# Half of a stage's matrices on other engines, and wider products, in a convolution with a fused feed-forward block

## The chip, the cores and the metric

The kernel runs on one core of a Trainium2 chip. Five engines work from their own instruction queues: PE (TensorE, matrix products into PSUM; its weight loads are shown as PEld), DVE (VectorE), ACT (ScalarE), POOL (GpSimd) and SP (SyncE), which here issues all transfers. A queue is worked in order; an instruction that waits holds up all behind it. The metric is the device time of one launch in microseconds (us), median of five runs.

## The reference

A long convolution, and a feed-forward block on its result (shapes: 4 batches, 12480 positions, 128 channels; 2048 hidden units; all float32):

```python
h_filt = (np.maximum(pos_emb @ w1, 0.0) @ w2) * np.exp(-0.01 * pos)[:, None]
u = x * v
y = irfft(rfft(u, n=2*S) * rfft(h_filt, n=2*S)[None])[:, :S]
x1 = (x * y).reshape(B*S, D)
h = x1 @ w_in
out = (h * np.cos(h)) @ w_out
```

## The kernel before

The transform of a batch is done in steps of matrix products: u = x * v and sums of it (u_units), a first step (f1_units, 64 blocks of two channels each), a second step with 48 pairs of matrices w, each followed by the product with the filter's transform (f2_units), and an inverse in two steps (i1_units, i2_units). Generators hand out pieces of this work, and `units` (L514) interleaves them: in the unit j it issues `before(j + ahead)`, the products of j, and the pieces of `after(j - 1)`.

The order of the opening, written out at L784 and below:

- The filter: 11 pieces of pos_emb are scaled (DVE, L331), turned and put through the first layer; then 30 times `filter_out` (two matmuls, a copy on ACT at L356, two sums on DVE at L359 into ftile). x * v of the first batch (first_u) is drawn along: a load of x and v (SP), the product in two halves on POOL or DVE (u_multiply, L390), and two sums, one on POOL and one on DVE (L396). x has three buffers, v two; v's buffer is free when both halves are done.
- f1 of the filter: 64 blocks of two matmuls (L402) whose results ACT or DVE evicts (f1_evict_filter; `share` is ACT's part), six pieces of which go by for each unit of first_u while that lasts. Afterwards the tables for the way back are made (inverse_tables: POOL makes the angles at L190 to L217, ACT the sines at L226, one step for every five pieces of f1) and stored.
- f1 of the first batch, beside which w_in is converted from 64-bit floats (L133 to L156).
- f2_both_units: each of the 48 pairs makes two matrices w, of the form even0 * a + even1 * b (`turn`: ACT makes the first term in a PSUM bank at L289, DVE multiplies and adds at L291), multiplies them with the batch and with the filter (L442, L445, L448), copies the filter's result to SBUF as h (ACT, L614), and multiplies by it: four products on DVE (L458, L460) and two sums on POOL (L461). w and h are stored to DRAM (wd, hd; SP) and read again for the other batches. w has two buffers, h three; w is made one pair ahead.
- i1 of the first batch, beside which w_out is converted and some of the matrices of the last step are made.

Then the main loop starts: the feed-forward block (L727 to L758) with the rest of the convolution drawn along, a piece whenever its share is due.

Of the kernel before, what the change touches and what calls it, by code (L numbers as in the profile page):

```python
# [30 lines left out]
def kernel(  # L31
# [46 lines left out]
    nc = tc.nc  # L78
# [30 lines left out]
    dram = ctx.enter_context(tc.tile_pool(name="dram", bufs=1, space=DRAM))  # L109
    hd = dram.tile([N1 // 2, N2, 2, 2, D], F32, name="hd")  # L110
    zd = dram.tile([NROWS, G, D], F32, name="zd")
# [140 lines left out]
    def inverse_tables(pool):  # L252

        t = Tables(pool, nc.gpsimd, 4)
        part = t.whole([P, 1], [[1, 1]], channel_multiplier=1, name="part")
        part4 = t.whole([P, 1], [[1, 1]], base=1, channel_multiplier=4, name="part4")
        step = t.whole([P, P], [[1, P]], name="step")
        mid = t.whole([P, P], [[1, P]], base=-MID, name="mid")
        cs, rows, tw_t = back_tables(pool)
        yield from t.sines(step, part, N2, [(cs[:, 0, 0:H + 1], 1), (cs[:, 1, 0:H + 1], 0)],  # L260
                           eighths=slice(0, H + 1, H))
        yield from t.sines(step[:, 1:H], part, N2,
                           [(cs[:, 0, H + 1:], 0), (cs[:, 1, H + 1:], 1)])
        yield from t.sines(step, part4, 4 * N1,
                           [(rows[:, i, :], q) for i, q in enumerate((0, 1, 2, 3))])
        yield from t.sines(mid, part4, TURN, [(tw_t[:, 0, :], 1), (tw_t[:, 1, :], 0)],
                           eighths=slice(H - 1, N2, H))
        t.finish(len(t.waiting))
        for kept, made in ((csd, cs), (rowsd, rows), (twd, tw_t)):
            nc.sync.dma_start(kept[:, :, :], made[:, :, :])  # L270

    def back_tables(pool):

        cs = pool.tile([N2, 2, N2], F32, name="cs")
        rows = pool.tile([N1, 4, R], F32, name="rows")

        tw_t = pool.tile([N1, 2, N2], F32, name="tw_t")
        return cs, rows, tw_t

# [157 lines left out]
    def f2_mm(ps, w, k1, i, filt=False):  # L437

        k = k1 + i
        pi = ps[0:N2, i * 2 * D:(i + 1) * 2 * D]  # L440
        if not filt:
            nc.tensor.matmul(pi, w[:, i, :], parts[0:KE, :, k], start=True, stop=True)  # L442
        elif k < KF:
            both = ftile[0:KE, :, k:k + N1 + 1:N1, :].rearrange("p b r i -> p r b i")
            nc.tensor.matmul(pi, w[:, i, :], both, start=True, stop=True)  # L445
        else:
            for r, src in enumerate((ftile[0:KE, :, k, :], above[0:KE, :, k - KF, :])):
                nc.tensor.matmul(pi[:, r * D:(r + 1) * D], w[:, i, :], src,  # L448
                                 start=True, stop=True)

    def f2_product(pool, ps, h, k1):

        y = parts[0:N2, :, k1:k1 + 2, :, :].rearrange("p r k b i -> p r b k i")
        uu, hh = (a.rearrange("p g r (b i) -> p r b g i", i=2) for a in (
            ps[0:N2, :].rearrange("p (g r d) -> p g r d", g=2, r=2), h[:, :, :, :]))
        t = pool.tile([N2, 2, CB, 2, 2], F32, name="t", bufs=1)
        for r, op in ((0, ALU.subtract), (1, ALU.add)):
            nc.vector.tensor_tensor(y[:, r], uu[:, 0], hh[:, r], op=ALU.mult)  # L458
            yield
            nc.vector.tensor_tensor(t[:, r], uu[:, 1], hh[:, 1 - r], op=ALU.mult)  # L460
            nc.gpsimd.tensor_tensor(y[:, r], y[:, r], t[:, r], op=op)  # L461
            yield
# [82 lines left out]

    def u_units(b, bufs, u, engine, side="left"):

        with tc.tile_pool(name="xv", bufs=bufs, side=side) as pool:
# [5 lines left out]
            def after(j, _):  # L554
                for half in range(2):
                    u_multiply(tiles[j], half, engine(j, half))
                    yield
                if j == H // UA - 2:
# [3 lines left out]

            yield from units(H // UA, U_STEPS, before, lambda j, ps, i: None, after, 3,
                             ahead=bufs - 2)

# [9 lines left out]
    def f2_units(bank):  # L575
        with tc.tile_pool(name="there", bufs=3) as pool:
            ws, hs = {}, {}

            def before(j):
                ws[j] = pool.tile([KE, 2, N2], F32, name="w")  # L580
                nc.sync.dma_start(ws[j][:, :, :], wd[j, :, :, :])
                hs[j] = pool.tile([N2, 2, 2, D], F32, name="h")
                nc.sync.dma_start(hs[j][:, :, :, :], hd[j, :, :, :, :])

            def mm(j, ps, i):
                if i == 0:
# [4 lines left out]
            yield from units(N1 // 2, F2_STEPS, before, mm,  # L591
                             lambda j, ps: f2_product(pool, ps, hs.pop(j), 2 * j), 4)

    def f2_both_units(bank):

        with tc.tile_pool(name="both", bufs=2) as pool:
            ws = {}

            def before(j):
                ws[j] = pool.tile([KE, 2, N2], F32, name="w")  # L600
                for i in range(2):
                    make_w(ws[j][:, i, :], 2 * j + i, half=bank)
                nc.sync.dma_start(wd[j, :, :, :], ws[j][:, :, :])
# [8 lines left out]
            def after(j, ps):  # L612
                h = pool.tile([N2, 2, 2, D], F32, name="h", bufs=3)
                nc.scalar.activation(h[:, :, :, :].rearrange("p g r d -> p (g r d)"),  # L614
                                     ps[1][0:N2, :], AF.Copy, scale=1.0 / M)
                nc.sync.dma_start(hd[j, :, :, :, :], h[:, :, :, :])
                yield from f2_product(pool, ps[0], h, 2 * j)

            yield from units(N1 // 2, F2_STEPS, before, mm, after, 4, ahead=1)

# [163 lines left out]
    with tc.manual_schedule():  # L784
        with tc.tile_pool(name="psum", bufs=8, space=PSUM) as psum, \
# [14 lines left out]
            with tc.tile_pool(name="layers", bufs=1, side="right") as pool:  # L800
# [8 lines left out]
                for i in range(1, NCH):  # L809
                    pes[i] = filter_load(pool, i)  # L810
                first_u = u_units(0, 3, slots[0:R, :, :, :],
                                  lambda j, half: nc.vector if half and j % 3 and j < 18
                                  else nc.gpsimd)
                next(first_u)
# [6 lines left out]
                for i in range(NCH + 1):  # L821
# [6 lines left out]
                    next(sines, None)  # L828
                    if i >= 4:
                        for _ in range(2):  # L830
                            next(first_u)
                for _ in sines:
# [5 lines left out]
            with tc.tile_pool(name="out", bufs=1, side="right") as pool:  # L838
                for j in range(H // 2):
                    filter_out(pool, bank, aT, ftile, j, w2_sb)  # L840
                    for _ in range(1 + (j % 3 == 0)):
                        next(first_u)
            f1 = f1_units(bank, ftile[0:FR, :, :, :], 0.53, f1_evict_filter)
            for _ in first_u:
                for _ in range(2):
                    next(f1)
# [26 lines left out]
            lpool = ctx.enter_context(tc.tile_pool(name="late", bufs=1))  # L873
            cs, rows, tw_t = back_tables(lpool)
            for kept, here in ((csd, cs), (rowsd, rows), (twd, tw_t)):
                nc.sync.dma_start(here[:, :, :], kept[:, :, :])
            for _ in f2_both_units(bank):
                pass
            first.close()

            wpool = ctx.enter_context(tc.tile_pool(name="weights", bufs=1))
            ident = wpool.tile([P, P], F32, name="ident")
            make_identity(nc, ident)
# [91 lines left out]
```

## Time and profile before

| | us |
|---|---|
| median of 5 runs | 3785.89 |
| the runs | 3781.93 to 3787.73 |
| profiled execution: device time | 3785.22 |
| its span, first to last instruction | 3783.4 |
| f1 of the filter begins | 64.09 |
| x * v of the first batch ends on POOL | 97.41 |
| f1 of the first batch: ACT's last eviction ends | 169.37 |
| i1 of the first batch begins | 272.83 |
| main loop's first feed-forward matmul | 345.29 |

In the lines of the profile, "out<-in" are the program's names of the tiles, then partitions x elements, "x" the number of instructions, busy time and the mean of one. The idle time of an engine is given with what ended it. "Busy" of PE is modelled, since matmuls are pipelined.

### The profile page before, as it was taken

The numbers are of one execution on the slowest core, as the hardware profiler recorded it, in microseconds if no ns is written. First come the engines' busy times: TensorE is split into PE (matmuls) and PEld (weight loads), VectorE is DVE, ScalarE is ACT, GpSimd is POOL, SyncE is SP. The second block draws the span as 40 slices with busy tenths as digits, with TensorE's granted clock in tenths as the row PEclk, the third lists the DMA queues.
The fourth block names the chain that finished last, engine by engine and source line by source line (L and its number), as shares of the span: only waits on it lengthen the run. The fifth ranks groups of instructions, "written<-read, shape, count | busy, mean of one in ns | idle before, by whom it ended". The sixth has DMA issues, their size and how long they took to land.

```text
span 3783.4 us, 47244 instructions
## 1 busy us (share of the span) xinstructions
PE 3701.4 (98%) x13546; PEld 2109.2 (56%) x13546; DVE 2769.3 (73%) x5658; ACT 2523.9 (67%) x4683; POOL 2588.6 (68%) x2342
## 2 busy tenths in 40 slices
PE   7898999999999999999999999999999999999999
PEld 6777555655466555555565556555566544444444
DVE  7887887688866777788766786788765566666666
ACT  5757776766665557666655567666664677777777
POOL 7667886588854665688745664788644577777776
PEclk9999999999999999999999999999999999999999
DMA  6253552022202650122103540122105200000000
GB/s 166 71 177 105 148 148 57 18 71 79 74 18 67 179 159 27 34 77 78 57 18 110 174 125 17 52 78 76 41 12 167 87 20 20 17 20 20 17 21 14
DMA packets 209500, 276.14 MB, mean 73 GB/s; under 512 B 17112, under 2 KB 146536, under 8 KB 209112
## 3 DMA queue, kind: packets, MB, share of 16 engines
q1 hardware_dynamic: 209239, 273.12, 24.9%
q8 instruction: 109, 1.79, 0.2%
q14 instruction: 152, 1.24, 0.1%
HBM read 193.64 MB, written 79.42 MB: 72 GB/s over the span
## 4 chain that ended last, share of the span: by engine, by line
PE 84%; POOL 7%; DVE 4%; ACT 2%; DMA 2%; issue 2%; SPq 0%; POOLq 0%; DVEq 0%; ACTq 0%
PE ph L727 31%; PE acc L752 27%; PE cv L752 5%; PE cv L491 5%; PE cv L466 4%; POOL f L736 4%; PE cv L402 3%; PE cv L442 3%; PE ph L126 2%; PE ps L402 1%; PE ps L442 1%; DMA tm<-td 1%; PE ps L466 1%; POOL tm L295 1%; DVE k L733 1%
## 5 line engine op out<-in xcount | busy, mean ns | idle before, releaser
L736 POOL TENSOR_TENSOR f<-a,k 128x512 f32<-128x512 f32 (+1 forms) x1568 | 1984.9, 1266 | 1054.2 <-DVE k L733 1053.2
L727 PE MATMUL ph<-at,w_in_sb 128*128 128x512 f32 (+1 forms) x3136 | 1599.9, 591 | 5.8 <-DVE gt L743 5.2
L730 ACT ACTIVATE a<-ph,quarter 128x512 f32<-128x512 f32 (+1 forms) x1568 | 1072.4, 684 | 760.7 <-PE ph L727 752.3
L752 PE MATMUL acc<-gt,w_out_sb 128*128 128x512 f32 (+1 forms) x2688 | 1374.4, 593 | 9.9 <-ACT ot L758 9.3
L743 DVE TENSOR_TENSOR gt<-ph,cs 128x512 f32<-128x512 f32 (+1 forms) x1568 | 1078.0, 687 | 317.2 <-ACT cs L741 289.2
L733 DVE TENSOR_SCALAR k<-a 128x512 f32<-128x512 f32 (+1 forms) x1568 | 769.1, 490 | 621.4 <-ACT a L730 604.1
L741 ACT ACTIVATE cs<-f 128x512 f32<-128x512 f32 (+1 forms) x1568 | 980.3, 625 | 329.3 <-POOL f L736 326.9
L752 PEld LDWEIGHTS acc<-gt,w_out_sb 128*128 128x128 f32 x2688 | 506.4, 189 | 662.3 <-issue 619.3
L727 PEld LDWEIGHTS ph<-at,w_in_sb 128*128 128x128 f32 x3136 | 554.4, 190 | 337.6 <-issue 267.2
L461 POOL TENSOR_TENSOR slots<-slots,t 120x256 f32<-120x256 f32 x384 | 311.3, 817 | 60.8 <-DVE t L460 38.8
L491 PEld LDWEIGHTS cv<-slots,tm 96*104 96x104 f32 x1920 | 239.8, 170 | 110.8 <-issue 79.9
L491 PE MATMUL cv<-slots,tm 96*104 96x128 f32 x1920 | 254.4, 275 | 10.8 <-DVE tm L291 4.9
L752 PE MATMUL cv<-gt,w_out_sb 128*128 128x512 f32 (+1 forms) x448 | 224.6, 584 | 0.7 <-DVE gt L743 0.7
L466 PEld LDWEIGHTS cv<-cs,slots 120*96 120x96 f32 x1536 | 176.8, 167 | 67.5 <-issue 65.6
L466 PE MATMUL cv<-cs,slots 120*96 120x120 f32 x1536 | 183.2, 266 | 0.0
L442 PE MATMUL cv<-slots,w 124*120 124x256 f32 x576 | 173.2, 381 | 0.0
L442 PEld LDWEIGHTS cv<-slots,w 124*120 124x120 f32 x576 | 103.7, 184 | 123.7 <-issue 110.8
L402 PEld LDWEIGHTS cv<-c,slots 104*124 104x124 f32 x768 | 132.6, 192 | 71.1 <-issue 58.3
L402 PE MATMUL cv<-c,slots 104*124 104x192 f32 x768 | 151.3, 327 | 4.8 <-DVE gt L743 3.5
L752 PEld LDWEIGHTS cv<-gt,w_out_sb 128*128 128x128 f32 x448 | 85.0, 190 | 104.4 <-issue 99.4
L390 DVE TENSOR_TENSOR xt<-xt,vt 104x256 f32<-104x256 f32 x177 | 138.8, 791 | 0.2
L476 DVE TENSOR_TENSOR slots<-cv,other 96x240 f32<-96x240 f32 x384 | 133.4, 393 | 4.2 <-ACT other L474 4.2
(129 smaller groups left out, 2579.3 us busy)
## 6 DMA issues: line engine op xcount, KB each, us to landing
h<-hd SPq DMA_DIRECT2D x144, 240.0 KB
tm<-td SPq DMA_DIRECT2D x96, 312.0 KB
xt<-in_x_dram SPq DMA_DIRECT2D x120, 208.0 KB
vt<-in_v_dram SPq DMA_DIRECT2D x120, 208.0 KB
xs<-in_x_dram SPq DMA_DIRECT2D x120, 208.0 KB
zd<-zs SPq DMA_DIRECT2D x119, 208.0 KB
zb<-zd SPq DMA_DIRECT2D x96, 256.0 KB
w<-wd SPq DMA_DIRECT2D x144, 116.2 KB
```

Source lines behind the costliest of these rows:

```text
L402: nc.tensor.matmul(ps[0:KE, i * 2 * N1:(i + 1) * 2 * N1], u[:, b, 0:KE, i], c1[0:u.shape[0], :, :].rearrange("p r k -> p (r k)"), start=Tr ...
L442: nc.tensor.matmul(pi, w[:, i, :], parts[0:KE, :, k], start=True, stop=True)
L461: nc.gpsimd.tensor_tensor(y[:, r], y[:, r], t[:, r], op=op)
L466: nc.tensor.matmul(ps[0:N1, (i * 2 + r) * N2:(i * 2 + r + 1) * N2], parts[0:N2, r, :, b, i], cs[:, r, :], start=True, stop=True)
L491: nc.tensor.matmul(ps[0:R, i * D:(i + 1) * D], t[:, i, r, :], slots[0:N1, :, place, :], start=(r == 0), stop=(r == 1))
L727: nc.tensor.matmul(ph[:, 0:m], w_in_sb[:, c * P:(c + 1) * P], ats[n][:, 0:m], start=True, stop=True)
L730: nc.scalar.activation(a[:, 0:m], ph[:, 0:m], AF.Identity, bias=quarter[:, 0:1], scale=INV_TWO_PI)
L733: nc.vector.tensor_scalar(out=k[:, 0:m], in0=a[:, 0:m], scalar1=ROUND, scalar2=ROUND, op0=ALU.add, op1=ALU.subtract)
L736: nc.gpsimd.tensor_tensor(f[:, 0:m], a[:, 0:m], k[:, 0:m], op=ALU.subtract)
L741: nc.scalar.activation(cs[:, 0:m], f[:, 0:m], AF.Sin, scale=TWO_PI)
L743: nc.vector.tensor_tensor(gt[:, 0:m], ph[:, 0:m], cs[:, 0:m], op=ALU.mult)
L752: nc.tensor.matmul(accs[n][:, 0:m], w_out_sb[:, c, :], gt[:, 0:m], start=(c == 0), stop=(c == NFC - 1))
```

## The change

In f2_both_units, the second matrix of each pair is made without DVE: ACT makes both terms in SBUF (the second in a tile `spare`), and POOL adds them. Matrices are made two pairs ahead instead of one, with three buffers of w; h has two buffers instead of three. The two halves of the product are one instruction each: the real part of the batch (or the imaginary part) is read twice, by a step of zero, and multiplied with both parts of h in one product of 512 elements; for this, the results of both matrices of a pair lie interleaved in PSUM and in h, so that the four elements of a pair of matrices and a pair of channels are neighbours. f2_units for the other batches keeps four products of 256, in the new layout. t has two buffers in the first case.

In first_u, the product x * v is one instruction for a unit (104x512) in place of two; DVE does those of the units 15, 19, 23 and 27, POOL the others (before, DVE did twelve halves among the first 18 units). The places where first_u is drawn are spread differently, and ACT's share of the filter's f1 is 0.58 instead of 0.53. The tables rows and tw_t for the last step are read back from DRAM after f2_both_units instead of ahead of it.

```diff
-        pi = ps[0:N2, i * 2 * D:(i + 1) * 2 * D]
+        pi = ps[0:N2, :].rearrange("p (r b g i) -> p g r b i", r=2, g=2, i=2)[:, i]
...
-    def f2_product(pool, ps, h, k1):
+    def f2_product(pool, ps, h, k1, whole):
+        y = parts[0:N2, :, k1:k1 + 2, :, :].rearrange("p r k b i -> p r b (k i)")
+        t = pool.tile([N2, 2, CB, 4], F32, name="t", bufs=1 + whole)
+        uu = ps[0:N2, :].rearrange("p (r b j) -> p r b j", r=2, j=4)
+        if whole:
+            for r, (dst, hh) in enumerate(((y, h[:, :, :, :]), (t[:, :, :, :], h[:, ::-1, :, :]))):
+                u = uu[:, r]
+                twice = bass.AP(tensor=u.tensor, offset=u.offset,
+                                ap=[u.ap[0], [0, 2], *u.ap[1:]])
+                nc.vector.tensor_tensor(dst, twice, hh, op=ALU.mult)
+                yield
         for r, op in ((0, ALU.subtract), (1, ALU.add)):
-            nc.vector.tensor_tensor(y[:, r], uu[:, 0], hh[:, r], op=ALU.mult)
-            yield
-            nc.vector.tensor_tensor(t[:, r], uu[:, 1], hh[:, 1 - r], op=ALU.mult)
+            if not whole:
+                nc.vector.tensor_tensor(y[:, r], uu[:, 0], h[:, r], op=ALU.mult)
+                yield
+                nc.vector.tensor_tensor(t[:, r], uu[:, 1], h[:, 1 - r], op=ALU.mult)
             nc.gpsimd.tensor_tensor(y[:, r], y[:, r], t[:, r], op=op)
             yield
...
-                for half in range(2):
+                for half in (0, 1) if halves else (slice(0, 2),):
                     u_multiply(tiles[j], half, engine(j, half))
...
     def f2_both_units(bank):
...
-                ws[j] = pool.tile([KE, 2, N2], F32, name="w")
-                for i in range(2):
-                    make_w(ws[j][:, i, :], 2 * j + i, half=bank)
+                ws[j] = pool.tile([KE, 2, N2], F32, name="w", bufs=3)
+                spare = pool.tile([KE, N2], F32, name="spare")
+                make_w(ws[j][:, 1, :], 2 * j + 1, spare=spare[:, :])
+                yield
+                make_w(ws[j][:, 0, :], 2 * j, half=bank)
+                yield
                 nc.sync.dma_start(wd[j, :, :, :], ws[j][:, :, :])
...
-                h = pool.tile([N2, 2, 2, D], F32, name="h", bufs=3)
+                h = pool.tile([N2, 2, CB, 4], F32, name="h")
...
-            yield from units(N1 // 2, F2_STEPS, before, mm, after, 4, ahead=1)
+            yield from units(N1 // 2, F2_STEPS, before, mm, after, 4)
...
-                                  lambda j, half: nc.vector if half and j % 3 and j < 18
-                                  else nc.gpsimd)
+                                  lambda j, half: nc.vector if j >= 15 and j % 4 == 3
+                                  else nc.gpsimd, halves=False)
...
-                    if i >= 4:
-                        for _ in range(2):
-                            next(first_u)
+                    if i >= 2:
+                        next(first_u)
...
-                    for _ in range(1 + (j % 3 == 0)):
+                    if j % 3:
                         next(first_u)
-            f1 = f1_units(bank, ftile[0:FR, :, :, :], 0.53, f1_evict_filter)
+            f1 = f1_units(bank, ftile[0:FR, :, :, :], 0.58, f1_evict_filter)
             for _ in first_u:
-                for _ in range(2):
+                for _ in range(3):
                     next(f1)
...
-            cs, rows, tw_t = back_tables(lpool)
-            for kept, here in ((csd, cs), (rowsd, rows), (twd, tw_t)):
-                nc.sync.dma_start(here[:, :, :], kept[:, :, :])
+            cs = third_table(lpool)
+            nc.sync.dma_start(cs[:, :, :], csd[:, :, :])
             for _ in f2_both_units(bank):
                 pass
             first.close()
             wpool = ctx.enter_context(tc.tile_pool(name="weights", bufs=1))
+            rows, tw_t = last_tables(wpool)
+            for kept, here in ((rowsd, rows), (twd, tw_t)):
+                nc.sync.dma_start(here[:, :, :], kept[:, :, :])
```

## The prediction

> **What bounds the kernel now.** I read the shares of each engine, the chain that ended last by line, busy time by stretch, and in the opening the waits and the order in time.
>
> ```profile
> PE 3701.4 (98%) x13546; PEld 2109.2 (56%) x13546; DVE 2769.3 (73%) x5658; ACT 2523.9 (67%) x4683; POOL 2588.6 (68%) x2342
> ```
>
> PE is full, and from 339 us on the chain is almost all PE. Apart from the layout of the products, the change touches only the first 339 us, so what it wins must be won there. Busy time by stretch (length, PE, PEld, DVE, ACT, POOL, clock, DMA share, GB/s):
>
> ```profile
> 31.20:64.09 32.89, 26.11 (x120) 19.52 (x121) 30.21 (x83) 11.04 (x30) 27.47 (x32) 0.95 0.59 173
> 64.09:97.40 33.31, 33.05 (x180) 32.45 (x180) 29.39 (x96) 25.52 (x113) 28.72 (x39) 0.90 0.51 145
> 97.40:120.28 22.88, 15.13 (x80) 12.80 (x80) 20.47 (x77) 11.99 (x52) 19.27 (x51) 0.96 0.04 13
> 120.28:169.37 49.09, 43.54 (x252) 42.62 (x252) 39.94 (x108) 44.06 (x133) 29.46 (x32) 0.95 0.23 67
> 205.00:267.00 62.00, 60.23 (x332) 48.01 (x332) 57.88 (x181) 36.70 (x88) 42.12 (x61) 1.00 0.61 176
> ```
>
> The filter's last layer (31 to 64) hangs on DVE, the next stretch on DVE and PE, the one from 97 on POOL, the one from 120 on ACT (44 of 49 us). Why from 97 on POOL, the order in time shows:
>
> ```profile
> 119.82 0.43 POOL L217 TENSOR_TENSOR turned<-moved,turned 96x120 f32<-96x120 f32 x1
> 120.28 0.30 ACT L226 ACTIVATE tw_t<-turned 96x120 f32<-96x120 f32 x1 [1.89 <-POOL turned L217]
> ...
> 121.80 4.45 PE L402 MATMUL ps<-c,slots 104*124 104x192 f32 x15 [7.05 <-ACT slots L410]
> ```
>
> POOL ends x * v of the first batch at 97.41, needs 22.8 us for the inverse tables, ACT waits for its last sine until 120.28, and PE stood 7.05 us behind ACT. So the end of x * v on POOL sets all that follows to 169.37.
>
> In the second step (f2_both_units, 169.4 to 272.8) DVE looks like the bound. But here is one pair:
>
> ```profile
> 207.27 0.24 SPq L603 DMA_DIRECT2D wd<-w  x1
> ...
> 208.67 0.59 DVE L291 SCALAR_TENSOR_TENSOR w<-even,tw_w,ps 124x120 f32<-124x120 f32 x2
> ...
> 209.29 0.24 SPq L603 DMA_DIRECT2D wd<-w  x1
> ...
> 210.68 0.59 DVE L291 SCALAR_TENSOR_TENSOR w<-even,tw_w,ps 124x120 f32<-124x120 f32 x2
> ```
>
> The store of w issued at 207.27 has its last completion at 210.56, and the matrix that reuses its buffer starts at 210.68; the store from 205.25 completes at 208.55, its successor starts at 208.67. From the sixteenth pair on the gap is 0.12 to 0.13 us nearly every time, which is also the gap after the visible stalls. So the stores hold the stage, whatever DVE does. In the trace's completions a store of w has one at 0.41 us and four at 2.7 to 3.3; a store of h one at 0.54 and fifteen at 2.4 to 3.6. A store of w thus runs on four DMA engines: 31 of its 124 packets each, one every 0.040 us; a store of h on fifteen, 8 packets each, one every 0.084. On the slowest engine w completes 1.38 after the h before it, and h 0.63 after the w before it: 2.01 us a pair, against 2.02 between issues. The mean DMA share of 0.61 hides this.
>
> [...]
>
> **The change, part by part.**
>
> *x * v with one product a unit.* POOL had 48 half products of 0.71 (34.1 us uncontended), DVE 12. Now 26 whole ones on POOL, 4 on DVE. No 104x512 product of two SBUF tiles is in this stage; nearest is POOL's 128x512 subtraction at 1.266 (33 us for 26), on DVE 104x512 at 0.680. So POOL hardly gains in work; DVE loses 12 x 0.41 and gains 4 x 0.68. What moves is the pace: in the last layer (30 filter_out) only 10 units come instead of 13. DVE there: 60 x 0.35 + 10 x 0.41 = 25 us, below PE's 26; so that layer takes 26 to 27 us plus the last pair's 1.3. It starts 0.6 earlier (one sum of u less stands between the filter's scalings), so f1 of the filter starts at about 58.5 instead of 64.09. But x * v itself runs at its own pace: load of v 3.05 us after its issue (86.31 to 89.40), then the product, two buffers: (3.1 + 1.3) / 2 = 2.2 us a unit at least, 2.35 with DVE's share (three evictions x 0.42 x 1.38 + a sum 0.43 + a quarter product), against 2.43 now. The sixteenth sum falls near 63.2 instead of 64.6, thirteen more units give 93.8, POOL's end 94.7: **-2.7** (bounds 0, same cadence, to -5, at 2.2).
>
> *Tables.* Same POOL work, so ACT resumes at 117.8. Only 7 of the sine steps are now placed among the filter's evictions, so these are done by then (two, 2.4 us of ACT, were left before), and ACT is free of sines; the other sines stand ahead of the first batch's evictions on ACT, and PE can run nine blocks ahead of them (eight banks) before it stops, as now. What ACT still has: 35 blocks x 1.06 + 8 conversions x 0.84 = 43.8, plus 2 idle (2.9 before): first step done at 163.6 instead of 169.3, **-5.7 together** (0 to -8). Share 0.58 instead of 0.53 is in these sums.
>
> *Second step.* Engines, per pair: DVE 2 x 0.68 + 0.335 = 1.70 by rows (six instructions, 2.34, spaced to 2.02 before); ACT 0.60 + 3 x 0.355 = 1.67; POOL 2 x 0.73 + one 124x120 sum, 0.43 by L217's 96x120, = 1.89; PE 1.75. All under 2.01, so the stores decide. Counted from ACT's end of the first step, E: the first store goes at E+1.4 (before E+1.0: a third ACT instruction), its packets 1.4 later; three stores of w follow at once, then the pipeline fills (PE 3.5 us to the first h, as now), and from the fifth w at E+10.6 the four engines are always fed: 44 x 1.38 + 43 x 0.63 = 87.8, E+98.4. Disturbed pairs add what they add now, 2.0 (intervals 2.49, 2.70, 2.29 and the like over 2.02). The last h needs the store two before it (two buffers instead of three), which lies behind the last w: 0.63 + 0.09 + copy 0.6 + products 1.3 + two sums 1.4 = 4.1. E+104.5; before 272.83 - 169.33 = 103.5. **+1** (bounds -7, if the packets alone counted, 1.91 a pair; +21, rival two). The waits of DVE on w (5.0 us in all) go; DVE's on POOL for t (1.6) too; h on its store is next, and behind it on ACT stand the three instructions of the w three pairs later, which has two pairs of slack. wd now waits for POOL and DVE on SP, and hd stands behind it; both have over 0.25 us in hand before the engines run dry.
>
> *Moved loads.* rows and tw_t are issued after the last h has landed, 0.3 us into the inverse step, ahead of w_in_sb and the raw pieces. They land 2.39 and 2.19 after issue; the first reader is ACT at 276.91, 4.1 in. w_in_sb and raw come 0.8 later; raw landed at 279.4 and DVE reads it at 282.23. **0**; without this cover, 1.2.
>
> *Layout.* PE now writes PSUM in runs of two elements; no matmul here does that. Reading runs of two from SBUF costs nothing: 256 columns of L442 come every 0.435, 1.70 ns each, as with L727's contiguous 512. The write side lies between 0 and a doubling; I take 0, as the reading row. The product over four contiguous elements stays at DVE's one-element pace (0.417), **0**.
>
> Sum: -5.7 + 1 = -4.7 on the profiled execution's 3785.22 (span 3783.4 and 1.8 around it): 3780.5. That execution is 0.67 under the median of the five runs, so for the median **3781**.
>
> **Rivals.**
> 1. *The stores are hidden.* The stage follows the packets (1.91) and the start fills sooner: 44 x (2.07 - 1.91) = -7, with the opening 3772.5. For: DVE is 93% busy. Against: the 0.12 us gap, the 1.38 between completions also when two w follow each other unblocked at the start.
> 2. *Slower: two buffers of h.* A pair takes at least (0.6 copy + 0.05 + landing + 0.09) / 2. Landing alone is 2.50 (1.6 a pair), behind w 3.58 (2.17, +5: 3784.5), at worst 4.29 (2.52, +21: 3800). It decides against the kernel by 0.2% from 3.95 on. Against it: between two stores of h that share a buffer the four engines have 3.4 us of other work anyway, so waiting adds nothing unless they idle.
> 3. *Strided PSUM writes cost PE.* Batches two to four have 288 such matmuls, 125 us: 10% is +12.5, 3793.5. Nothing in the trace speaks for it, nor excludes it.
> 4. *No change*: x * v keeps 2.43 a unit and the tables end at 120: 3784 to 3787.
>
> **How the numbers follow.** Forecast 0.58 (own range 3776 to 3786), rival one 0.17, two 0.13, three 0.05, four 0.07. The measurement tells 0.2%, 7.6 us: faster means under 3778.3. That holds for nearly all of rival one and a quarter of the forecast's cases: 0.30; slower, over 3793.5: two's upper part and three, 0.10; same 0.60. The range 3770 to 3790 leaves out rival one's best and the slower cases.
>
> **What would show it.** f1 of the filter starting near 58.5; the last IOTA on POOL near 95; ACT's first w at 163.6; intervals of wd still 2.01 to 2.05 with DVE idle in them; the inverse step starting near 268. Wrong if intervals of wd fall to 1.9 (one), if ACT waits on hd with the intervals over 2.2 (two), or if L442 in the later batches lengthens (three).

## The result, and the profile after

The changed kernel takes 3793.06 us (median of 25 runs, 3788.39 to 3797.04) against 3786.25 for the kernel before (43 runs beside it): 6.8 us longer, a ratio of 1.0016 with a 95% interval of 1.0011 to 1.0022. The forecast was 3781, its range ended at 3790. The profiled execution took 3795.57, with a span of 3793.8; it is one of the longer ones.

The first row of the page of the changed kernel: VectorE lost 17 us of work and 172 instructions, GpSimd and ScalarE gained 13 each.

```profile
PE 3704.2 (98%) x13546; PEld 2112.6 (56%) x13546; DVE 2752.0 (73%) x5486; ACT 2537.3 (67%) x4751; POOL 2601.9 (69%) x2368
```

Busy time by stretch (length, PE, PEld, DVE, ACT, POOL, clock, DMA share, GB/s); the borders are the same events as before, but for 107.00: x * v ends on GpSimd at 105.0 and its first table instruction starts at 106.43.

```profile
33.98:62.88 28.90, 26.13 (x121) 19.57 (x121) 26.86 (x70) 11.04 (x30) 21.77 (x21) 0.99 0.46 133
62.88:107.00 44.12, 40.93 (x223) 39.17 (x224) 41.89 (x119) 35.05 (x155) 27.08 (x33) 0.93 0.49 142
107.00:129.23 22.23, 10.87 (x63) 9.74 (x61) 13.40 (x47) 9.16 (x39) 18.69 (x47) 0.88 0.04 12
129.23:176.17 46.94, 41.39 (x228) 40.21 (x228) 37.54 (x102) 41.81 (x122) 29.46 (x32) 0.90 0.24 71
205.00:267.00 62.00, 60.22 (x318) 46.78 (x317) 46.00 (x91) 42.46 (x121) 54.83 (x91) 1.00 0.59 178
```

The filter's last layer is 4 us shorter, but starts 2.8 us later. From there to GpSimd's first table instruction it is 43.6 us where it was 33.4, with VectorE busy in 95% of that stretch. The tables, from that instruction to the last sine, take what they took (22.8 us, 22.8 before), and what follows a little less (46.9, 49.1 before), only later. The second step shows the idle VectorE that was forecast (46.0 of 62 us; 57.9 before), and no speed from it. The order in time shows what the late tables bring:

```profile
129.23 0.30 ACT L226 ACTIVATE tw_t<-turned 96x120 f32<-96x120 f32 x1 [1.89 <-POOL turned L217]
129.56 0.31 SPq L270 DMA_DIRECT2D twd<-tw_t  x1
130.64 5.80 PE L404 MATMUL ps<-c,slots 104*124 104x192 f32 x17 [11.98 <-ACT slots L412]
131.28 1.31 SPq L173 DMA_DIRECT2D raw<-in_moe_w_in_dram  x3
134.81 0.29 DVE L133 TENSOR_SCALAR power<-raw 128x256 uint32<-128x256 uint32 x1 [13.96 <-DMA raw<-in_moe_w_in_dram]
```

The last sine ends 9 us later than before (120.28), TensorE stands 12.0 us behind ScalarE instead of 7.1, and VectorE, which did not wait there before, stands 14.0 us for the raw words of the feed-forward weights, whose loads come behind the tables' stores. The first batch's first step ends at 176.17 on ScalarE instead of 169.37. From there to the first matmul of the third step it is 106.1 us (103.5 before); from that matmul to the end 3511.5 (3510.6). So nearly all of the loss arises ahead of the third step.

### The profile page after: what moved, and what is told of

It reads as the page before. It is cut to its first block, busy times and chain, and to the rows that moved or that the text cites. A ratio compares the mean times of both kernels' runs of the same rounds, so it can differ in the third digit from the quotient of the medians.

```text
span 3793.8 us, 47221 instructions
## 1 busy us (share of the span) xinstructions
PE 3704.2 (98%) x13546; PEld 2112.6 (56%) x13546; DVE 2752.0 (73%) x5486; ACT 2537.3 (67%) x4751; POOL 2601.9 (69%) x2368
## 4 chain that ended last, share of the span: by engine, by line
PE 81%; POOL 7%; DVE 4%; DMA 3%; ACT 2%; issue 2%; SPq 0%; POOLq 0%; DVEq 0%; ACTq 0%
PE ph L740 31%; PE acc L765 26%; PE cv L765 5%; PE cv L501 4%; PE cv L476 4%; POOL f L749 4%; PE cv L404 3%; PE cv L445 3%; PE ph L126 2%; DMA tm<-td 1%; DMA hd<-h 1%; POOL slots L471 1%; PE ps L476 1%; ACT cs L754 1%; POOL tm L297 1%
## 5 line engine op out<-in xcount | busy, mean ns | idle before, releaser
L471 POOL TENSOR_TENSOR slots<-slots,t 120x256 f32<-120x256 f32 x384 | 311.1, 816 | 32.7 <-DVE t L470 16.5
L486 DVE TENSOR_TENSOR slots<-cv,other 96x240 f32<-96x240 f32 x384 | 133.5, 393 | 4.1 <-ACT other L484 4.1
L392 DVE TENSOR_TENSOR xt<-xt,vt 104x256 f32<-104x256 f32 (+1 forms) x169 | 133.8, 799 | 0.3 <-DMA vt<-in_v_dram 0.3
```

## The experiments

The opening theory: x * v of the first batch ends later, and tables, raw words and first step with it. The rival: the second step makes the loss. This table holds, for one profiled execution of each kernel, the first matmul of the filter's last layer, of the filter's first step, the last matmul of batch 0's first step, the first of the second and of the third step; then the difference of the medians to the runs of the kernel before on the same chip. An opening varies from one execution to the next: in the five kernels with the whole new opening (changed, e2, e4, e6, e7) batch 0's first step ends at 166.6 to 172.1. The profiled execution also need not be a typical one: it lies 2.5 us above the median of its kernel's runs in the changed kernel and 3.0, 3.9 and 5.3 below it in e2, e3 and e4. So single rows tell less than groups.

| kernel | last layer | filter's first step | batch 0's first step ends | second step | third step | median less before |
|---|---|---|---|---|---|---|
| before | 31.2 | 64.1 | 165.2 | 170.2 | 272.8 | |
| changed | 34.0 | 62.9 | 172.0 | 177.6 | 282.3 | +6.8 |
| e1 old opening | 30.7 | 63.5 | 165.8 | 171.5 | 275.5 | +2.4 |
| e2 new opening alone | 31.5 | 60.8 | 166.6 | 171.6 | 274.6 | +2.8 |
| e3 two f1 a step | 31.4 | 59.4 | 169.7 | 175.4 | 278.7 | +5.9 |
| e4 stores by ScalarE | 32.3 | 60.9 | 168.5 | 174.2 | 277.8 | +7.8 |
| e5 more steps in the last layer | 31.8 | 66.2 | 166.1 | 171.8 | 276.9 | +2.9 |
| e6 earlier raw loads | 35.8 | 64.7 | 172.1 | 177.8 | 282.0 | +5.0 |
| e7 cut store | 32.5 | 61.6 | 171.3 | 177.0 | 274.6 | +1.1 |
| e8 old opening, cut store | 30.7 | 63.6 | 165.2 | 170.9 | 268.5 | -6.2 |
| e9 before, cut store | 31.8 | 64.8 | 167.0 | 172.0 | 274.0 | -2.0 |
| e10 late draws | 30.2 | 58.9 | 166.8 | 172.5 | 276.8 | +1.7 |
| e11 two halves | 31.9 | 59.6 | 165.4 | 171.1 | 275.0 | +3.3 |
| e12 cut store, both draws | 29.6 | 65.6 | 166.2 | 171.9 | 270.9 | -3.0 |

The 95% intervals of the medians' ratios reach about 3.4 us to each side for e1 to e12, 2.1 for the changed kernel; a difference between two of these kernels under some 4 us is therefore not clear of the noise.

### e1 and e2: one half each

e1 is the changed kernel with these parts as before:

```diff
-                                  lambda j, half: nc.vector if j >= 15 and j % 4 == 3
-                                  else nc.gpsimd, halves=False)
+                                  lambda j, half: nc.vector if half and j % 3 and j < 18
+                                  else nc.gpsimd)
...
-                    if i >= 2:
-                        next(first_u)
+                    if i >= 4:
+                        for _ in range(2):
+                            next(first_u)
...
-                    if j % 3:
+                    for _ in range(1 + (j % 3 == 0)):
                         next(first_u)
-            f1 = f1_units(bank, ftile[0:FR, :, :, :], 0.58, f1_evict_filter)
+            f1 = f1_units(bank, ftile[0:FR, :, :, :], 0.53, f1_evict_filter)
             for _ in first_u:
-                for _ in range(3):
+                for _ in range(2):
                     next(f1)
```

> The changed kernel with the opening put back (x * v in half products, draws, shares and engine choice as before); the second step and the moved table loads stay changed. Opening theory (the loss arises ahead of the second step): x * v ends on GpSimd near 97.4 us, the first step of batch 0 ends on ScalarE near 169.4, the second step still takes the changed kernel's 106.5 us to the first matmul of the third step, which therefore starts near 276; time 3789 us (3787 to 3791). Rival, the second step makes the loss: third step near 282, time 3793.

e2 is the kernel before with the changed side of that diff.

> The kernel before with the new opening alone. Opening theory: x * v ends near 106 us, the last sine of the inverse tables near 129, batch 0's first step ends on ScalarE near 176, the second step takes 103.5 us as before, third step near 279.7; time 3793 us (3791 to 3795). Rival, the second step makes the loss: 3786 us (3784 to 3788) with batch 0's first step ending near 169.

Measured: e1 3790.16, ratio 1.0007 (0.9998 to 1.0015); e2 3790.56, ratio 1.0010 (1.0001 to 1.0019). Both lose, each less than the whole, and the two together (5.2 us) make up the 6.8 within the uncertainty. So neither theory holds alone: it seems that the opening costs something, and the second step too, though e1's 2.4 is not clear of the noise by itself. The opening cost less in e2 (2.8) than the 6.8 that the changed kernel's profile had suggested. By e7 less e8, which differ in the opening alone and ran on one chip, it is 7.2 us; by the changed kernel less e1, 4.4. That it costs something is shown; its size lies between these.

### e3: fewer matmuls beside x * v

```diff
             for _ in first_u:
-                for _ in range(3):
+                for _ in range(2):
                     next(f1)
```

> The changed kernel with two instead of three first-step units of the filter drawn at each step of x * v, so four matmul pairs beside a unit of x * v where there were six. Theory that x * v is held at the pace of the filter's first step (15 units left, 2.87 us each, with TensorE busy 31.6 of 33 us): 15 units at about 2.35 us end near 98 us, tables' last sine near 121, batch 0's first step ends near 170; time 3787 us (3785 to 3790). Rival, the whole products themselves are slow (loads of v into two buffers come too late, and sums wait): x * v still ends at 104 or later and the time stays at 3793.

Measured: 3793.64, ratio 1.0015 (1.0007 to 1.0024). x * v did end sooner: the last sums on VectorE and GpSimd start at 96.2 and 96.3, the last sine at 120.2. And nothing was won that is clear of the noise. The filter's first step, first matmul to last, in e3 and then in the changed kernel:

```profile
L404 PE MATMUL ps<-c,ftile x256: 326/326/682, 59.4 to 126.7; 96*124 96x192 f32 x128
```

```profile
L404 PE MATMUL ps<-c,ftile x256: 325/327/652, 62.9 to 113.7; 96*124 96x192 f32 x128
```

In e3 TensorE is busy for 28.2 of the 33 us from 64 to 97 (31.6 in the changed kernel), with four pairs of matmuls to a unit. What x * v gained, the filter's own first step lost. So the end of x * v is not by itself what the opening hangs on, as the prediction and my first theory had it. The next theory is that it hangs on how much of x * v is left when the filter's first step begins.

### e5: more of x * v inside the filter's last layer

```diff
                     filter_out(pool, bank, aT, ftile, j, w2_sb)
-                    if j % 3:
-                        next(first_u)
+                    next(first_u)
```

> The changed kernel with a step of x * v at every one of the 30 iterations of the filter's last layer instead of at two of three: 20 units of x * v are issued when the filter's first step begins, 10 are left, where 15 were left in the changed kernel and 11.3 in the one before. Theory that the opening loses because more units are left beside the filter's first step, each with six matmul pairs (2.87 us): x * v ends 10 units later instead of 15, at 88 to 95 us although the last layer gets 2 to 4 us longer, the tables end near 114 to 118 and batch 0's first step by 170; time 3788 us (3786 to 3791). Rival, the opening is bound by the sum of the work and not by that order: the last layer lengthens by as much as x * v gains, batch 0's first step does not end sooner, time 3793.

Measured: 3788.96, ratio 1.0010 (1.0002 to 1.0019), 2.9 over the kernel before instead of 6.8; with the intervals above, that gain of 3.9 us is at the edge of the noise. By the draws, 15 units are left in the changed kernel, 11.3 in the old opening, 10 here. Last layer and the two first steps, in us, from the table:

| units left | kernels | last layer | filter's and batch 0's first step | sum |
|---|---|---|---|---|
| 15 | changed, e2, e4, e6, e7 | 29.0 | 107.9 | 136.9 |
| 11.3 | before, e1, e8, e9 | 32.9 | 101.8 | 134.7 |
| 10 | e5 | 34.4 | 99.9 | 134.3 |

By these groups, a unit taken out of the last layer saves about 1.1 us there and costs about 1.6 behind it: moving 3.7 of them won 3.9 us and lost 6.1. That would be 2.2 of the opening's loss, and e5 agrees. But the three later kernels speak against the number of units as the whole cause: e10, with 15 left, makes 28.7 + 107.9 = 136.6, and e12, which differs from it here by having 10 left, 36.0 + 100.6 = 136.6, no less; e11, with 15 left but half products, makes 27.7 + 105.8 = 133.5, the least of all. So the units left are a likely part of it and not shown as its cause.

### e4 and e6: the raw words behind the tables' stores

e4 issues the three stores on ScalarE's queue:

```diff
         for kept, made in ((csd, cs), (rowsd, rows), (twd, tw_t)):
-            nc.sync.dma_start(kept[:, :, :], made[:, :, :])
+            nc.scalar.dma_start(kept[:, :, :], made[:, :, :])
```

> The changed kernel with the three stores of the inverse tables issued by ScalarE instead of SyncE, so that the raw feed-forward weights' loads no longer stand behind them. Theory that SyncE's order adds to the loss: the raw loads are issued before 125 us (131.3 in the changed kernel), VectorE's 14.0 us wait for them shrinks under 4, batch 0's first step ends between 171 and 174 us instead of 176.2; time 3789 to 3791. Rival, only GpSimd's late tables matter: batch 0's first step still ends near 176 and the time stays at 3793.

Measured: 3795.55, ratio 1.0018 (1.0009 to 1.0026): no gain. The order in time of e4:

```profile
124.74 0.30 ACT L226 ACTIVATE tw_t<-turned 96x120 f32<-96x120 f32 x1 [1.90 <-POOL turned L217]
125.75 0.43 ACTq L270 DMA_DIRECT2D twd<-tw_t  x1
127.83 1.30 SPq L173 DMA_DIRECT2D raw<-in_moe_w_in_dram  x3
```

With no store before them on SyncE, the raw loads still wait until 2.1 us after the last store was issued, and VectorE waited 15.0 us for them. So SyncE's order does not hold them. The weights' buffers lie where the tables were, and the tables are free only when their stores have landed: that fits, but was only argued.

e6 builds the tables in memory of the other side and puts the last store behind the first raw loads:

```diff
+        tw_t = kept_pool.tile([N1, 2, N2], F32, name="tw_t")
...
         for kept, made in ((csd, cs), (rowsd, rows), (twd, tw_t)):
+            if made is tw_t:
+                yield REST
             nc.sync.dma_start(kept[:, :, :], made[:, :, :])
...
-            with tc.tile_pool(name="tables", bufs=1) as pool:
+            with tc.tile_pool(name="tables", bufs=1, side="right") as pool:
...
-                   [(wind[:, c], w) for c, w in in_pieces])
+                   [(wind[:, c], w) for c, w in in_pieces], lambda pool: sines)
```

> The changed kernel with the tables built in memory of the other side and the last table's store behind the first raw weight loads on SyncE, so that these need not wait for the last sine and its store. Theory that VectorE's wait of 14 us for the raw words adds to the loss: they are issued about 5 to 7 us earlier against the last sine than in the changed kernel (1.8 us behind it there), the wait falls below 8 us, and the step from batch 0's first matmul to its last (58.1 us in the changed kernel, 51.3 before) shortens by 2 to 4 us; time 3790 us (3788 to 3792). Rival, ScalarE's sines alone hold TensorE (11.98 us wait) and VectorE's wait lies beside that: no change, 3793.

Measured: 3791.0, ratio 1.0013 (1.0004 to 1.0021). The raw loads came 0.3 us behind the last sine's start instead of 2.0, not the 5 to 7 sooner that I had meant: something else held them to the tables. VectorE's wait was 12.2 us instead of 14.0. What that wait costs by itself stays open; no run took it away.

### e10 and e11: why the last layer starts late

The last layer starts at 30.7 to 31.8 in the four kernels with the old opening and at 31.5 to 35.8 in the five with the new one (means 31.1 and 33.2; as in the two tables above, without e3, e5 and e10 to e12). Two candidates: VectorE's sums, placed earlier in its order, and the long products on GpSimd. VectorE and GpSimd in the order of time in the changed kernel:

```profile
18.34 0.26 DVE L217 TENSOR_TENSOR turned<-moved,turned 124x96 f32<-124x96 f32 x1
...
18.73 1.60 POOL L392 TENSOR_TENSOR xt<-xt,vt 104x512 f32<-104x512 f32 x1 [15.43 <-DMA vt<-in_v_dram]
19.11 1.28 DVE L210 TENSOR_SCALAR moved<-prod 124x96 f32<-124x96 f32 x1
20.40 0.72 POOL L398 TENSOR_TENSOR slots<-xt 104x256 f32<-104x256 f32 x1
20.50 0.69 DVE L213 TENSOR_SCALAR turned<-moved 124x96 f32<-124x96 f32 x1
21.09 1.26 POOL L392 TENSOR_TENSOR xt<-xt,vt 104x512 f32<-104x512 f32 x1
21.23 1.19 DVE L215 TENSOR_SCALAR turned<-turned 124x96 f32<-124x96 f32 x1
```

The same three instructions on another table of that size, just before, with GpSimd idle:

```profile
16.24 0.21 DVE L210 TENSOR_SCALAR moved<-prod 124x96 f32<-124x96 f32 x1
17.85 0.21 DVE L213 TENSOR_SCALAR turned<-moved 124x96 f32<-124x96 f32 x1 [1.39 <-ACT even L226]
18.09 0.21 DVE L215 TENSOR_SCALAR turned<-turned 124x96 f32<-124x96 f32 x1
```

Beside GpSimd each ends within 0.1 us of the end of the GpSimd instruction that ran beside it (20.39 and 20.33, 21.19 and 21.12, 22.42 and 22.35). Behind these tables stand the scalings of the filter's input.

e10 takes the ten steps of x * v beside the hidden layer later:

```diff
-                    if i >= 2:
-                        next(first_u)
+                    if i >= 4:
+                        for _ in range(1 + (i >= 10)):
+                            next(first_u)
```

> The changed kernel with the ten steps of x * v beside the filter's hidden layer taken from its fifth round on (two in the last two rounds) instead of from the third. Theory that VectorE's sums, placed among the scalings of the filter's input, hold the hidden layer: its last matmul ends at 29.5 to 30.5 us (30.0 to 34.4 in the seven runs of the new opening, 29.4 to 29.9 in the three of the old), the last layer starts near 31, batch 0's first step ends 2 us sooner; time 3791 us (3789 to 3792). Rival, the hidden layer is late because GpSimd's products of 1.27 us hold VectorE wherever its sums stand: no change, 3793.

Measured: 3788.41, ratio 1.0007 (0.9998 to 1.0016). Its hidden layer:

```profile
L346 PE MATMUL ps<-peT,w_sb x22: 566/575/1022, 9.0 to 28.9; 128*128 128x480 f32 x22
```

In the changed kernel that line reads 8.9 to 32.7. The last layer started at 30.2, sooner than with the old opening, and the loss shrank to 1.7. In e12, which has the same edit, it started at 29.6. There GpSimd's first product started at 18.81, just as these tables were done; in e3, with the early draws, it was 18.84, the tables were done too, and the last layer started at 31.4. So the place of the sums accounts for about 2 us of the late start. The two latest starts, 34.0 and 35.8, belong to the changed kernel and e6, where the products met the tables; e2's first product, at 19.04, met two of the three (0.63 and 0.78 us), and its last layer started at 31.5. No execution with the late draws met them, so that part is left to the next experiment. The time won, 5.1 us against the changed kernel, is more than the 2 us expected, within the uncertainty.

e11 keeps the order and issues each whole product as two:

```diff
-                for half in (0, 1) if halves else (slice(0, 2),):
+                for half in range(2):
                     u_multiply(tiles[j], half, engine(j, half))
-                    yield
+                    if halves or half:
+                        yield
```

> The changed kernel with each whole product of x * v issued as two products of half the size, one straight behind the other on the same engine, steps and order unchanged. Theory that a long GpSimd product holds VectorE for its whole length (table operations of 0.21 us took up to 1.28 us where products ran beside them): VectorE's operations of the forward tables take at most about 0.95 us, the hidden layer ends by 31 us; GpSimd gives up 26 times 0.18 us; time 3791 to 3794. Rival: lengths unchanged.

Measured: 3790.06, ratio 1.0008 (0.9999 to 1.0017), last layer from 31.9. The tables' instructions kept their 0.20 to 0.28 us, but in this execution the first load of v landed at 19.0, when the tables were done, so nothing met and the length was not put to the test. e1 shows such a meeting: there GpSimd's half products started at 17.69, and L210 and L213 took 0.73 and 0.58 us where the changed kernel's took 1.28 and 0.69; its last layer started at 30.7, but it has the old order too. In e1:

```profile
19.59 0.73 DVE L210 TENSOR_SCALAR moved<-prod 124x96 f32<-124x96 f32 x1
20.43 0.58 DVE L213 TENSOR_SCALAR turned<-moved 124x96 f32<-124x96 f32 x1
```

Behind the last layer the long products did meet VectorE, and this was overlooked at first. VectorE has one sum for each unit (L398, L396 in the kernel before), which alone takes 0.41 to 0.43 us. All 30 of them in the kernel before, the changed kernel and e11 (duration in ns, least, median and most):

```profile
L396 DVE TENSOR_TENSOR slots<-xt x30: 407/427/927, 21.3 to 96.4; 104x256 f32<-104x256 f32 x30
L398 DVE TENSOR_TENSOR slots<-xt x30: 411/787/1489, 23.2 to 105.8; 104x256 f32<-104x256 f32 x30
L398 DVE TENSOR_TENSOR slots<-xt x30: 411/427/979, 20.4 to 98.9; 104x256 f32<-104x256 f32 x30
```

One pair of them in the changed kernel:

```profile
102.87 1.27 POOL L392 TENSOR_TENSOR xt<-xt,vt 104x512 f32<-104x512 f32 x1 [0.21 <-DMA vt<-in_v_dram]
103.17 1.25 DVE L398 TENSOR_TENSOR slots<-xt 104x256 f32<-104x256 f32 x1
```

From the filter's first step on, ten of the changed kernel's sixteen sums took over 0.7 us, and each of the ten ended 0.28 us behind the GpSimd instruction that it had met, nine times a whole product. On the mean a sum took 0.71 to 0.89 us there in the five kernels with the new opening, 0.59 to 0.72 in the four with the old one, 0.56 in e11. So the long products do take time on VectorE where it is the full engine. How much of the kernel's time that is, e11's 3790 against 3793 does not tell clear of the noise.

### e7, e8 and e9: the store of w in two pieces

The 124 partitions of w go to DRAM in one store; here 120 and 4:

```diff
-                nc.sync.dma_start(wd[j, :, :, :], ws[j][:, :, :])
+                for p in (slice(0, N2), slice(N2, KE)):
+                    nc.sync.dma_start(wd[j, p, :, :], ws[j][p, :, :])
```

> The changed kernel with each matrix store of the second step cut in two, 120 rows and 4 rows. Theory that the second step is bound by its stores (124 packets on 4 engines, 2.01 us a pair): the 120 rows lie on 15 engines, the interval between matrix stores falls from 2.01 to about 1.91 us, which is GpSimd's work, or lower, the second step shortens by 4 to 6 us; time 3788 us (3786 to 3790). Rival, an engine bounds the step at the same pace: interval stays at 2.01, time stays at 3793.

> The kernel with the old opening and the changed second step, each matrix store cut into 120 and 4 rows. By the store theory 4 to 6 us faster than the old opening with uncut stores, which took 2.4 us more than the kernel before: 3783 to 3786 us where the kernel before takes 3787. Rival: as with uncut stores, 3789 to 3790.

> The kernel before with each matrix store of the second step cut into 120 and 4 rows. Theory A, its second step is bound by VectorE (74.9 of 80 us busy, 2.02 us a pair): interval at least 1.9 us, time 3784 to 3787. Theory B, it stood at the stores just as the changed kernel does (interval 2.02 us in both, three buffers of h or two): the interval falls to VectorE's 1.89 us, 60 pairs by 0.13 us make 7 us at the most and some 5 likely, time 3780 to 3783; then most of what the cut store brought would not be the changed second step's, and the changed kernel's interval of 2.01 would be throughput of the four engines and not the latency of a store with two buffers.

How many DMA engines the 120 rows lie on, no run shows: fifteen is an estimate from h's stores of 120 rows in the kernel before, which have fifteen completions at 2.4 to 3.6 us.

Measured: e7 (changed kernel) 3787.09, ratio 1.0004 (0.9995 to 1.0013); e8 (e1 with the cut) 3779.88, ratio 0.9983 (0.9974 to 0.9992); e9 (kernel before) 3784.72, ratio 0.9997 (0.9988 to 1.0006). ScalarE and the stores in the second step of the changed kernel, in the order of time:

```profile
206.22 0.60 ACT L627 ACTIVATE h<-ps 120x512 f32<-120x512 f32 x1 [0.60 <-DMA hd<-h]
206.43 0.24 SPq L616 DMA_DIRECT2D wd<-w  x1
206.85 0.32 SPq L629 DMA_DIRECT2D hd<-h  x1
208.22 0.60 ACT L627 ACTIVATE h<-ps 120x512 f32<-120x512 f32 x1 [0.58 <-DMA hd<-h]
208.45 0.24 SPq L616 DMA_DIRECT2D wd<-w  x1
```

and of e7:

```profile
207.06 0.66 SPq L617 DMA_DIRECT2D wd<-w  x2
207.82 0.32 SPq L630 DMA_DIRECT2D hd<-h  x1
207.92 0.60 ACT L628 ACTIVATE h<-ps 120x512 f32<-120x512 f32 x1 [0.34 <-DMA hd<-h]
208.67 0.68 SPq L617 DMA_DIRECT2D wd<-w  x2
```

The changed kernel issues a store of h every 2.02 us (median from 190 to 260 us), e7 every 1.87, e8 every 1.80; a store of h lands 3.31 us after its issue there, 2.46 and 2.45 here. From the last matmul of batch 0's first step to the third step it is 109.8 us with the changed step and the whole store (mean of the changed kernel, e1, e3 to e6, e10, e11; 109.0 to 110.8), 103.8 with the cut one (e7, e8, e12; 103.3 to 104.7), 107.5 in the old step (before, e2, e9; 107.0 to 108.0). So the changed second step lost 2.3 us with the whole store and wins 3.7 with the cut one; e8 went past the 3783 to 3786 us expected. The busy times in e8 show what comes close next:

```profile
205.00:267.00 62.00, 56.95 (x343) 48.59 (x341) 48.97 (x96) 43.54 (x122) 57.28 (x95) 1.00 0.67 189
```

GpSimd has 57.3 of 62 us, and ScalarE still waits for stores of h (19.0 us in 31 waits from 180 to 260). And e9 sets the prediction's reading of the kernel before right, as its theory A had it: the cut brought a store of h to 2.40 us from 3.60, and ScalarE's waits turned from that store to TensorE's results, and still the interval stayed at 2.03. Waits from 180 to 260 us in the kernel before, then in e9, and e9's busy times:

```profile
ACT h L614 <- DMA hd<-h: 28.6, 36, 1.2
```

```profile
ACT h L615 <- PE ps L445: 14.5, 21, 1.1
ACT h L615 <- DMA hd<-h: 3.4, 3, 1.3
```

```profile
205.00:267.00 62.00, 60.99 (x335) 48.62 (x336) 58.43 (x184) 37.95 (x91) 43.28 (x61) 1.00 0.66 181
```

The four kernels make a square. Old step and whole store 2.02 us, changed step alone 2.01 (e1), cut store alone 2.03 (e9), both 1.80 (e8). Stores and engines stood at the same pace in the old step, and taking one away left the other; that the engine is VectorE (58.4 of 62 us busy in e9) is likely, since the changed step takes its work away. Whether the changed kernel's 2.02 is the throughput of the four DMA engines that the prediction read from the four late completions of a store of w (2.01 by its sum of 1.38 and 0.63) or the turn of two h buffers (copy 0.60, some 0.1, landing 3.31, halved: 2.0) is not settled: cutting the store eases both, and no run has the changed step with three buffers of h.

### e12: the pieces together

The changed kernel with the edits of e5, e7 and e10.

> The changed kernel with the late draws, a step of x * v at every iteration of the filter's last layer, and the cut matrix store together. By the terms measured one by one: cut store 6 us, more steps in the last layer 4 us, late draws 2 us, so 3793 less 12 is 3781 (3778 to 3784), level with the old opening and the cut store (3780). Rival, the opening's parts do not add: 3783 to 3787.

Measured: 3783.73, ratio 0.9990 (0.9982 to 0.9999). Batch 0's first step ends at 166.2, no sooner than with e5 or e10 alone (166.1, 166.8): these two do not add. The opening in its old form with half products (e8, 165.2) is as good or better, and e8 is the fastest version, 6.2 us below the kernel before and some 13 below the changed one.

## Why the prediction was wrong

**x * v, the step that failed.** The prediction said that "x * v itself runs at its own pace", 2.35 us a unit, and ends on POOL at 94.7, which made -2.7. It ended there at 105.0 in the changed kernel and at 99.9 to 106.7 in e2, e4, e6 and e7. Three things in that step were wrong.

- The count. From the sixteenth of 30 sums fourteen units are left, not thirteen, so that its own pace would have given 97.0 and a gain of 0.4. The sum at 64.6 that it compared with is the eighteenth of the kernel before: twelve units took 31.8 us there, 2.65 each and not 2.43.
- The pace. The last fourteen units took 2.50 to 2.76 us each in the five executions, no faster than before. The sum of 2.35 has VectorE's evictions, but VectorE's sum of u in it at 0.43 us, which took 0.71 to 0.89 on the mean beside GpSimd's long products; with the changed kernel's 0.86 it is 2.78, where 2.68 was measured. The four whole products given to VectorE also stand behind its evictions: GpSimd waited 4.4 to 10.8 us for them.
- The start. It started the last layer 0.6 us sooner; it started 2.1 later on the mean, in part since sums on VectorE moved up among the scalings (e10).

GpSimd's sums of the kernel before, the eighteenth and the last, and of the changed kernel, the sixteenth and the last:

```profile
64.61 0.97 POOL L396 TENSOR_TENSOR slots<-xt 104x256 f32<-104x256 f32 x1 [0.42 <-DVE xt L390]
...
96.44 0.97 POOL L396 TENSOR_TENSOR slots<-xt 104x256 f32<-104x256 f32 x1
```

```profile
66.65 0.73 POOL L398 TENSOR_TENSOR slots<-xt 104x256 f32<-104x256 f32 x1 [2.85 <-DVE xt L392]
...
104.21 0.79 POOL L398 TENSOR_TENSOR slots<-xt 104x256 f32<-104x256 f32 x1
```

In the changed kernel that is 3.4 us by the sixteenth sum (66.65, not 63.2), 2.35 by the unit left out and 4.7 by the pace, together the 10.4 from 93.8 to 104.2. And e3 shows that the end of x * v was not the right thing to look at: it came 8 us sooner there and won nothing. By five executions against four, batch 0's first step ended 4.3 us later on TensorE instead of 5.7 sooner on ScalarE: 2.1 by the last layer's start, and 2.2 in the last layer and the two first steps. How these 2.2 divide between the units left and the long products is open.

**Tables and first step behind it.** "Same POOL work" held (22.8 us from the first table instruction to the last sine, as before), and from the last sine to ScalarE's end 46.9 us passed where the prediction's sum made 45.8. The sign of the step came from its start alone. TensorE's longer wait and VectorE's new one for the raw words had not been seen; the words' loads stood in the profile of before at 122.34, just behind the last store.

**Second step.** The mechanism was right: the stores decided, the interval stayed at 2.02 with VectorE idle, and rival one's interval (stores hidden, 1.91) is what e7 and e8 reach or pass by cutting the store. The size was +2.3 where the sum made +1. 0.7 of the 2.3 lies at the start, 5.6 to 5.7 us from the last matmul to the first instead of 5.0, and about 1.4 behind the last store of w, from whose issue it is 6.6 to 7.4 us to the third step instead of 5.4 to 5.6. The term that was too small is the time to the landing of the last w, at E+100.4 by the sum and E+102.2 in the changed kernel; the rest behind it, 4.1 by the sum, took 3.9. The claim that the stores hold the old step "whatever DVE does" fell with e9: both held it.

**Rivals two, three and four.** Slower intervals by two buffers of h did not come (2.02). The strided PSUM writes cost nothing that shows: the later batches' products, 381 ns on the mean before and after, read

```profile
L442 PE MATMUL cv<-slots,w 124*120 124x256 f32 x576 | 173.2, 381 | 0.0
L445 PE MATMUL cv<-slots,w 124*120 124x256 f32 x576 | 173.1, 381 | 0.0
```

No change in x * v (rival four) would have been nearer than the forecast, but it had no loss either. No case joined a loss in the opening to the slower second step, and it was that sum, 4.3 + 2.3 = 6.6 against 6.8 measured, that ended past the range. That the two agree so closely is partly luck, since the medians put the opening at 2.8, 4.4 or 7.2 us.

**Moved loads.** At nothing, as forecast: from the third step's first matmul to the end it is 3508.1 to 3513.8 us in all fourteen kernels, with no order in it.

## What to carry to other kernels

When work is moved from beside one stage to beside the next, price it in the stage that receives it, by the engine that is full there, and not by the mover's own pace: here x * v took 2.65 us a unit beside the first step before the change, and that row could have been read. Count an instruction of the full engine at what it takes beside its neighbours, 0.7 to 0.9 us here, and not at what it takes alone, 0.43. VectorE, freed in a stage that the stores also limited, gave nothing here until the store was cut (2.01 us a pair in e1, 1.80 in e8); look at the number of partitions of each store, since 124 rows as 120 and 4 turned a loss of 2.3 us into a gain of 3.7. And with an opening that varies by 5 us from one execution to the next, one pair of profiles shows where to look, not how much.

## What the runs showed of the hardware

In the changed kernel a short VectorE instruction beside a GpSimd instruction took up to six times its length (L210, 0.21 and 1.28 us), and the three of the tables ended within 0.1 us of it. VectorE's sums of two tiles took up to 1.49 us instead of 0.43, and each that took longer than 0.43 ended 0.28 us behind a GpSimd instruction. A whole product took 1.27 us on GpSimd, less than two halves of 0.73 (medians, changed kernel and e11), and the longest times on VectorE stand beside whole products: L210 and L215 took 1.28 and 1.19 us there, L210 and L213 0.73 and 0.58 in e1, which has halves. The traces show these lengths and ends; what holds VectorE there they do not show. How much of it showed went with the time at which GpSimd's first product started: with the new order beside the hidden layer and whole products, the two executions in which GpSimd's first product started at 17.9 and 18.7 us had their last layer start at 35.8 and 34.0, the five others (e2 to e5 and e7), with 18.8 to 19.9, at 31.4 to 32.5.
